# Two exchanges of an FFT convolution: from moves inside SBUF to stores and loads through DRAM, with both frequency halves in one transform and a new plan of the order

## The chip, the cores and the metric

The kernel runs on one core of one Trainium2 chip. The metric is the device time of one execution in microseconds (us). A kernel is run several times, in rounds with the kernel before on the same chip; each execution also lists the mean clock that was granted to TensorE, as a share of full speed. Engines: PE is TensorE's matmul side, PEld its weight loads (they overlap), DVE is VectorE, ACT is ScalarE, POOL is GpSimd, SP is SyncE. All DMAs of this kernel are issued from SP's one queue, strictly in program order; "SPq" in the profile is that queue's issuing.

## The reference, cut to what matters

```python
def _A_ref(q, k, v, shift_k, ssm_k, ssm_D):        # S = 2048, D = 640
    # kv = (4-tap causal shift filter of k) * v
    kv_f = rfft(pad(kv, S));  kf_f = rfft(pad(ssm_k, S))     # length 2S, along the sequence
    y = irfft(kv_f * kf_f)[:, :S, :] + kv * ssm_D
    return q * y

def _B_ref(x, w1, w2, w3, w4):
    h = gelu(layernorm(x) @ w1)          # then a shift by one or two tokens, by column group
    x1 = x + shifted(h) @ w2
    return x1 + gelu(layernorm(x1) @ w3) @ w4      # w3: 640 x 1536

return g * a + (1 - g) * b               # a = _A_ref(x, ...), b = _B_ref(x, ...), x = A_q
```

The change touches the long convolution in `_A_ref`. The dense matmuls of `_B_ref` stay as they are and are there for PE to work on while the convolution waits.

## The kernel before

The 2048 tokens lie as 128 partitions (`P`) x 16 (`T1`); `D` is 640 channels and `DH` is half of them. A transform is done in two matmul stages. The first stage (`F1`) works on each of the 16 slices; then the data must be exchanged between partitions, because the second stage (`M3`, a 128x128 block matrix) needs, on one partition, what lay on 16 others. In a partition index `(a q)` of the first stage, `a` goes from 0 to 7 and `q` from 0 to 15; after the exchange the partitions are `(a, t)`.

Half of the channels (`dh`) and half of the frequencies (`h`) are taken at a time, so there are eight transforms: four of the filter (r = 0 to 3; results go to `HD` in DRAM), four of the data (r = 4 to 7; multiplied with the filter's and brought back by one stage into `VR`). After each pair of data transforms, an inverse needs a second exchange. Both exchanges are DMAs from SBUF to SBUF:

```python
    def gx(r):                       # first exchange: 16 moves of 80 KB in each of 8 transforms
        stage = (RA, RB)[r % 2]
        for k in range(T1):
            w = [k_s2[r - 1, k // 2]] if r else k_cj + k_f1
            k_gx[r, k] = dma(lambda k=k: GRt[:, k, :],
                             lambda k=k: stage.rearrange("(a q) t d -> a q t d", a=8)[:, k],
                             P * 640, 640, evs + w)          # evs: all eight evacuations of stage 1

    def inverse(dh):                 # second exchange: 16 moves of 160 KB for each of 2 inverses
        vdeps = [k_v[r, kp] for r in (4 + 2 * dh, 5 + 2 * dh) for kp in range(T1 // 2)]
        for tp in range(T1 // 2):
            vb = G.buf("pv")                                  # three slots
            for j in range(2):
                k_vx[dh, t1] = dma(lambda vb=vb, j=j: PV[:, vb.slot, j],
                                   lambda t1=t1: VR.rearrange("(a q) t h d -> a q t (h d)", a=8)[:, t1],
                                   P * 1280, 1280, vdeps + ns, take=[vb] if j == 0 else [])
            ...                                               # then the inverse's matmuls and evacuation
```

The order of instructions isn't written by hand. The kernel builds a graph of all operations, and a list scheduler, run when the kernel is built, plans it with cost constants and with a pair of priorities for each group of operations (`WANTED`). What it plans is the order in which each engine gets its instructions. The constants for DMAs:

```python
    def dma(self, nbytes, packet, deps, fn, take=(), give=()):
        n = self.add({"D": (0.6, 0.6)}, deps, lambda e: fn(), take, give)          # us to issue
        n.bytes = -(-nbytes // packet) / 16.0 * (0.03 * -(-packet // 4096) + packet / 27000.0)
    ...
                    if opts == "D" and len(dmas) >= 8 and dmas[-8] > now + 1e-9:   # eight in flight
                        continue
    ...
                    line = max(now + 1.9, line) + n.bytes     # every packet is shared by 16 engines
```

Of the kernel before, what the change touches and what calls it, by code (L numbers as in the profile page):

```python
# [30 lines left out]
class Graph:  # L31
# [21 lines left out]
    def dma(self, nbytes, packet, deps, fn, take=(), give=()):  # L53
        n = self.add({"D": (0.6, 0.6)}, deps, lambda e: fn(), take, give)
        n.bytes = -(-nbytes // packet) / 16.0 * (0.03 * -(-packet // 4096) + packet / 27000.0)
        return n
# [23 lines left out]
    def forward(self):  # L80
# [19 lines left out]
        while placed < len(nodes):  # L100
            while True:
# [25 lines left out]
                if n.bytes is not None:  # L127
                    line = max(now + 1.9, line) + n.bytes
                    fin = line + 0.7
                    dmas.append(fin)  # L130
# [36 lines left out]
    "tables": (668, 1861), "loads": (3010, 3397.5), "hT": (1054, 1150.5), "LN1": (1024.5, 1172.5),  # L167
    "W1": (851, 1958.5), "W1.0": (337, 568), "W1.1": (526, 633), "W1.2": (263, 1091), "W1.3": (213.5, 699),
    "gate": (287, 3792.5), "mixsh": (902.5, 1653.5), "W2": (504, 741.5), "ks": (1289, 2357), "I1": (463.5, 2277.5),
    "p0.1": (-20, 674), "p0.gx": (115.5, 1589.5), "p1.1": (2353, 3097.5), "p0.2": (79, 136), "p1.gx": (240.5, 432.5),  # L170
    "p2.1": (863.5, 950.5), "p1.2": (110.5, 958.5), "p2.gx": (71, 358), "p3.1": (64, 1032.5), "p2.2": (395, 975),
    "p3.gx": (297, 1420.5), "p4.1": (371, 969), "p3.2": (252.5, 1391), "p4.gx": (1472, 1553), "p5.1": (722, 1661),
    "p4.hh": (770, 1452.5), "p4.2": (1240, 1290), "p5.gx": (-20, 254.5), "p6.1": (63.5, 287.5),
    "p5.hh": (2300.5, 3013), "p5.2": (132, 300), "p6.gx": (1391.5, 2568), "inv0": (1209.5, 2253.5),
    "p7.1": (58, 174.5), "p6.hh": (2391, 2893.5), "p6.2": (432.5, 679), "p7.gx": (617.5, 3276.5),
    "p7.hh": (696, 1575.5), "p7.2": (454, 1231), "inv1": (550.5, 1330.5), "LN2": (1022.5, 1104.5),
    "LN2.0": (1284.5, 1692.5), "W3.0": (75, 243), "W4.0": (503, 2717), "LN2.1": (347, 952.5), "W3.1": (3658, 4180),
    "W4.1": (592.5, 2133), "LN2.2": (232.5, 368.5), "W3.2": (426, 2444.5), "W4.2": (1684.5, 1911.5),
    "LN2.3": (2004.5, 3650.5), "W3.3": (461, 634), "W4.3": (2785.5, 3746.5), "final": (3243.5, 4779.5),
# [11 lines left out]
def kernel(  # L191
# [16 lines left out]
    nc = tc.nc  # L208
# [26 lines left out]
    HT = big.tile([P, 2, T1, DH], BF16, name="HT")  # L235
    R3 = big.tile([P, T1, 2, DH], BF16, name="R3")
    R5 = big.tile([P, 2 * T1 * DH], BF16, name="R5")
    R4 = big.tile([P, FT * D], BF16, name="R4")
    GR = big.tile([P, T1 * DH], BF16, name="GR")
# [5 lines left out]
    XY = big.tile([P, 2, D], BF16, name="XY")  # L245
    XS = big.tile([P, 2, 2, DH], BF16, name="XS")
    PV = big.tile([P, 3, 2, 2, DH], BF16, name="PV")
    HST = big.tile([P, 2, 4, DH], BF16, name="HST")
    HD = dram.tile([4, P, T1 * DH], BF16, name="HD")
    PS = [psp.tile([P, 2, 512], F32, name="ps%d" % i) for i in range(4)]  # L250

    KN = R3.rearrange("p t e d -> p t (e d)")
    VR = R3
    HN = R5.rearrange("p (a t2 t1) -> p a t1 t2", a=DT, t1=T1)
    HNl = R5.rearrange("p (a t) -> p a t", a=DT)
    GRt = GR.rearrange("p (t d) -> p t d", t=T1)
    RA = R5[:, 0:T1 * DH].rearrange("p (t d) -> p t d", t=T1)
    RB = R5[:, T1 * DH:].rearrange("p (t d) -> p t d", t=T1)
    HH = HT
# [6 lines left out]
    CJB = GR[:, 0:4 * D]  # L266
# [10 lines left out]
    NANG = [R11[:, 4 * T1 * 130:4 * T1 * 130 + 2048].bitcast(I32), GR[:, 4 * D:4 * D + 2048].bitcast(I32)]  # L277
# [13 lines left out]
    G.pool("hst", 2)  # L291
    G.pool("xnt", 2)
    G.pool("gtp", 5)

    def cact(n):
        return (0.11 + n / 1300.0, 0.28 + n / 1300.0)
# [7 lines left out]
    def pe(cols, n=1):  # L304
        return n * max(0.066, 0.000472 * cols)
# [88 lines left out]
    for g in range(4):  # L394
# [3 lines left out]
        for j in range(4):  # L398
# [11 lines left out]
            parts.append(act(P, [k_s16, k_wv, k_small] + before, f_sin))  # L410
        k_and = dvec(0.7, parts, lambda g=g: nc.vector.tensor_scalar(
            out=NANG[g % 2], in0=NANG[g % 2], scalar1=8191, scalar2=None, op0=ALU.bitwise_and))
        k_f1.append(act(1024, [k_and], lambda g=g: nc.scalar.activation(
# [3 lines left out]

    M3 = cons.tile([P, 3, P], BF16, name="M3")
    prow = gtile(1, I32)
    k_prow = pool(0.1, [], lambda: nc.gpsimd.iota(prow, pattern=[[1, 1]], base=0, channel_multiplier=1))  # L420
    tr = gtile(3)
    tri = tr.bitcast(I32)

    def make_tr():
        for i, bits in enumerate((15, 48, 64)):
            nc.vector.tensor_scalar(out=tri[:, i:i + 1], in0=prow, scalar1=bits, scalar2=None, op0=ALU.bitwise_and)
        nc.vector.tensor_copy(out=tr, in_=tri)

    k_tr = dvec(0.4, [k_prow], make_tr)
    ck1, k_ck1 = iof(3 * P, ([[0, 24], [1, 16]], 0, 0))  # L430
    cof, k_cof = iof(3 * P, *(([[stp, 2], [0, 64]], b0, 0) for (stp, b0) in ((12, 12), (4, 12), (4, 8))))
    crm = gtile(3 * P)

    def make_crm():
        for m, val in enumerate((4.0 / 64, 8.0 / 64, 0.0)):
            nc.gpsimd.memset(crm[:, m * P:(m + 1) * P], val)

    k_crm = pool(0.85, [], make_crm)
    ckl, k_ckl = iof(P, ([[0, 2], [16, 4], [0, 16]], 0, 0))
# [3 lines left out]
    def make_an():  # L443
        nc.vector.scalar_tensor_tensor(out=an, in0=ck1, scalar=tr[:, 0:1], in1=cof, op0=ALU.mult, op1=ALU.add)
        nc.vector.scalar_tensor_tensor(out=ani, in0=crm, scalar=tr[:, 2:3], in1=an, op0=ALU.mult, op1=ALU.add)
        nc.vector.tensor_scalar(out=ani, in0=ani, scalar1=15, scalar2=None, op0=ALU.bitwise_and)
        nc.vector.tensor_scalar(out=ckl, in0=ckl, scalar1=tr[:, 1:2], scalar2=None, op0=ALU.is_equal)

    k_an = dvec(1.5, [k_tr, k_ck1, k_cof, k_crm, k_ckl], make_an)
    k_m3s = act(3 * P, [k_an], lambda: nc.scalar.activation(out=ck1, in_=ani, func=ACT.Sin, scale=PI / 8, bias=BPI[:]))  # L450

    def make_m3():
        for m in range(3):
            nc.vector.tensor_tensor(out=M3[:, m, :], in0=ck1[:, m * P:(m + 1) * P], in1=ckl, op=ALU.mult)
# [38 lines left out]
    for k in range(DT):  # L493
        k_w1m.append(pool(0.43, [l_w1], lambda k=k: nc.gpsimd.tensor_copy(
            out=W1M[:, k, :].rearrange("p (g c) -> p g c", g=4),
            in_=W1[:, k, :].rearrange("p (g c) -> p g c", g=4)[:, :, P:CG])))
    k_cj = []
    for j in range(4):
        k_cj.append(G.add({"G": (1.36, 1.43), "V": (0.47, 0.55)}, [l_cj], lambda e, j=j: (
# [38 lines left out]
    for p in range(8):  # L538
        ns = []
        for s in (2 * p, 2 * p + 1):  # L540
# [4 lines left out]
            ns.append(dvec(0.97, [l_q[s]], f_st))  # L545
# [117 lines left out]
    l_w3a = dma(lambda: W3[:, 0:3], lambda: w3v[:, 0:3], 3 * P * 3072, 3072, k_w1)  # L663
# [56 lines left out]
    for s in range(T1):  # L720
# [15 lines left out]
        k_x1.append(dvec(0.93, [k_w2[s]], f_x1, give=[b]))  # L736
        k_sq.append(G.add({"A": (0.8, 0.97)}, [k_x1[s]] + [n for (_, _, n) in k_mix], lambda e, s=s: nc.scalar.activation(  # L737
            out=JK, in_=QX[:, s, :], func=ACT.Square, accum_out=SQS[:, s:s + 1])))
    l_w3b = dma(lambda: W3[:, 3:5], lambda: w3v[:, 3:5], 2 * P * 3072, 3072, k_w2)
# [24 lines left out]
    l_w4 = dma(lambda: W4[:], lambda: B_w4.rearrange("(k p) e -> p k e", p=P), Fh * D * 2, 1280, kprev)  # L764

# [15 lines left out]
    k_gx = {}  # L781
    k_s2 = {}
    k_hd = {}
    k_pq = {}
    k_v = {}
    k_vx = {}
    k_inv = {}
    k_hh = {}
    k_s1 = {}
    l_qr = []  # L790
    stage_done = {}

    def pass1(r):
        G.tag = 'p%d.1' % r
        dh, h = divmod(r % 4, 2)
        ds = slice(dh * DH, (dh + 1) * DH)
        stage = (RA, RB)[r % 2]
        war = [k_gx[r - 2, k] for k in range(T1)] if r >= 2 else k_hn_free
        evs = []
        k_s1[r] = []  # L800
        for tp in range(T1 // 2):
            b = G.buf("ps")

            def f(b=b, tp=tp):
                for j in range(2):
                    t1 = 2 * tp + j
                    dt = r < 4 and t1 == 0
                    src = HT[:, dh, t1, :] if r < 4 else KV[:, t1, ds]
                    nc.tensor.matmul(P32(b)[:, j, 0:DH], lhsT=F1[:, t1, h, :], rhs=src, start=True, stop=not dt)  # L809
                    if dt:  # L810
                        nc.tensor.matmul(P32(b)[:, j, 0:DH], lhsT=F1[0:1, 0, h, :], rhs=DROW[:, ds], start=False,
                                         stop=True)
            deps = [k_f1[tp // 2]] + (k_ht[dh] + [l_d] if r < 4 else [k_ks[4 * dh + tp // 2]])
            t = ten(pe(DH, 2), deps + war, f, take=[b])
            k_s1[r].append(t)
            evs.append(evac(2 * DH, PSD, [t], lambda tp=tp: stage[:, 2 * tp:2 * tp + 2, :],
                            lambda b=b: P32(b)[:, :, 0:DH], give=[b]))
        stage_done[r] = evs

    def gx(r):  # L820
        G.tag = 'p%d.gx' % r
        stage = (RA, RB)[r % 2]
        evs = stage_done[r]
        for k in range(T1):
            w = [k_s2[r - 1, k // 2]] if r else k_cj + k_f1
            k_gx[r, k] = dma(lambda k=k: GRt[:, k, :], lambda k=k: stage.rearrange("(a q) t d -> a q t d", a=8)[:, k],
                             P * 640, 640, evs + w)

    def pass2(r):
        G.tag = 'p%d.2' % r  # L830
        h = r % 2
        for kp in range(T1 // 2):
            b = G.buf("ps")

            def f(b=b, kp=kp):
                for j in range(2):
                    nc.tensor.matmul(P32(b)[:, j, 0:DH], lhsT=M3[:, 0, :], rhs=GRt[:, 2 * kp + j, :], start=True,  # L837
# [219 lines left out]
```

## Time and profile before

| kernel before | |
|---|---|
| median of three executions | 315.14 us (310.18 to 316.18) |
| profiled execution | span 312.4 us, granted clock 0.961 |
| all later executions beside other kernels | 309 to 315 us, mostly labelled fast |

In profiles a tile has the program's name with a buffer number: here `R_72` holds the first stage's results (`RA`, `RB`) and `R_71` holds `VR`; `ps_85` to `ps_88` are PSUM buffers. The page of the profile has these lines (busy time, share of the span and instructions of each engine; the DMA engines' busy share and the rate in the third part):

```profile
span 312.4 us, 4773 instructions
...
PE 250.7 (80%) x1690; PEld 153.5 (49%) x1690; DVE 181.0 (58%) x343; ACT 182.2 (58%) x261; POOL 45.9 (15%) x127
...
DMA packets 41745, 54.73 MB, mean 175 GB/s; under 512 B 4986, under 2 KB 34427, under 8 KB 41722
...
q1 hardware_dynamic: 41722, 54.44, 62.5%
...
PE 38%; DMA 27%; SPq 10%; ACT 10%; DVE 8%; issue 5%; POOL 1%; ACTq 0%; DVEq 0%
```

No engine is full, and the chain of waits (last line) runs through PE for only 38% of the span. DMA and the queue's issuing hold 37% of it. The next lines give what the queue does: for each kind of transfer its count, and the shortest, median and longest time in ns to issue one.

```profile
L337 SPq DMA_DIRECT2D GR<-R_72 x128: 589/599/3366, 45.4 to 254.5; - x128
L337 SPq DMA_DIRECT2D PV<-R_71 x32: 589/622/1667, 203.4 to 299.1; - x32
...
L337 SPq DMA_DIRECT2D HD<-HST x16: 321/452/936, 55.3 to 156.3; - x16
```

The exchange moves (`GR`, `PV`) take 0.59 us at the least, the plain store of a whole tile (`HD`) 0.32 us. PE's longest waits for DMAs of the exchanges (us in total, times, longest):

```profile
PE ps_87 L913 <- DMA PV<-R_71: 9.9, 4, 6.8
PE ps_88 L913 <- DMA PV<-R_71: 5.2, 3, 3.3
PE ps_86 L837 <- DMA GR<-R_72: 3.5, 3, 2.4
...
PE ps_86 L913 <- DMA PV<-R_71: 3.0, 1, 3.0
...
PE ps_85 L913 <- DMA PV<-R_71: 1.2, 2, 1.0
```

The four `PV` lines are 19.3 us: PE stands before the inverse. And the chain of waits near the end shows how (start us, length us, what): one move lands after 5.52 us, two matmuls run, and the queue issues the next moves.

```profile
276.76 5.52 DMA PV<-R_71
...
282.32 0.45 PE ps_88 L913 x2
282.77 0.58 SPq L337
...
283.41 0.60 SPq L337
```

Of each line the first number is the window, the second its length, and the last three are the granted clock, the busy share of the 16 DMA engines, and GB/s:

```profile
46.00:52.50 6.50, 5.83 (x59) 3.41 (x57) 6.36 (x13) 4.95 (x7) 0.00 (x0) 1.00 0.42 87
247.00:255.00 8.00, 8.00 (x47) 4.42 (x46) 2.48 (x3) 6.26 (x9) 0.00 (x0) 1.00 0.45 105
271.00:281.00 10.00, 8.06 (x48) 4.47 (x46) 2.23 (x4) 1.50 (x3) 0.00 (x0) 1.00 0.42 100
```

In these stretches the busy share stays at 0.42 to 0.45 and the rate at about 100 GB/s.

### The profile page before, as it was taken

How to read it: one execution, taken by the hardware profiler on the slowest of the kernel's cores; microseconds unless marked ns; L12 is line 12 of the kernel's file. 1: busy time of each engine (PE TensorE's matmuls, PEld its weight loads, DVE VectorE, ACT ScalarE, POOL GpSimd, SP SyncE). 2: the span in 40 equal slices, each digit the busy share in tenths (PEclk: the TensorE clock that was granted, in tenths of full speed). 3: DMA queues.
4: the chain of work that ended last, by engine and by line, in shares of the span. 5: the costliest groups of instructions: out<-in, count | busy, mean ns of one | idle time of the engine just before them, and what ended most of it. 6: DMA issues, size and time to landing. Idle time of an engine off the chain costs nothing.

```text
span 312.4 us, 4773 instructions
## 1 busy us (share of the span) xinstructions
PE 250.7 (80%) x1690; PEld 153.5 (49%) x1690; DVE 181.0 (58%) x343; ACT 182.2 (58%) x261; POOL 45.9 (15%) x127
## 2 busy tenths in 40 slices
PE   0297788889969896989959799965879999977845
PEld 0283345446646552546636455532546566645522
DVE  7899779969876899341313553211358145336733
ACT  8677888766856995886848688510215677410000
POOL 5877300003674310000000000000000000000000
PEclk9997999999997999999989999996999999999987
DMA  7999805657455299695585899647641836045561
GB/s 252 405 316 370 309 7 105 154 163 185 87 154 173 102 239 264 171 316 159 145 221 143 203 219 261 150 113 210 163 102 35 196 77 166 14 119 157 147 187 52
DMA packets 41745, 54.73 MB, mean 175 GB/s; under 512 B 4986, under 2 KB 34427, under 8 KB 41722
## 3 DMA queue, kind: packets, MB, share of 16 engines
q1 hardware_dynamic: 41722, 54.44, 62.5%
q8 instruction: 13, 0.21, 0.3%
q14 instruction: 10, 0.08, 0.1%
HBM read 30.31 MB, written 7.86 MB: 122 GB/s over the span
## 4 chain that ended last, share of the span: by engine, by line
PE 38%; DMA 27%; SPq 10%; ACT 10%; DVE 8%; issue 5%; POOL 1%; ACTq 0%; DVEq 0%
DMA GR<-R_72 11%; SPq L337 10%; DMA PV<-R_71 8%; PE ps_86 L987 5%; ACT R_72 L327 4%; DMA R_73<-in_B_w_dram 3%; PE ps_85 L1004 3%; PE ps_85 L987 3%; DVE BST L543 2%; DMA HT<-HD 2%; PE ps_86 L1004 2%; PE ps_88 L726 2%; PE ps_87 L631 2%; PE ps_86 L726 2%; PE ps_87 L1004 1%
## 5 line engine op out<-in xcount | busy, mean ns | idle before, releaser
L1004 PEld LDWEIGHTS <-R_79 128*128 128x128 bf16 x384 | 39.1, 102 | 20.1 <-DMA R_73<-in_B_w_dram 1.5
L862 DVE TENSOR_TENSOR PV<-XS,HT 128x1280 bf16<-128x1280 bf16 x32 | 25.9, 824 | 29.5 <-ACT XS L327 27.0
L987 PEld LDWEIGHTS <-R_77 128*128 128x128 bf16 x240 | 23.3, 98 | 24.5 <-issue 4.0
L987 PE MATMUL ps_86<-XNT,R_77 128*128 128x512 bf16 x100 | 24.8, 379 | 3.6 <-ACT HST L329 3.1
L993 ACT ACTIVATE R_79<-ps_86 128x1024 bf16<-128x1024 f32 x10 | 10.2, 1023 | 25.8 <-PE ps_86 L987 20.9
L756 DVE TENSOR_TENSOR R_73<-R_71,R_73 128x1280 bf16<-128x1280 bf16 (+3 forms) x32 | 23.9, 757 | 0.1
L580 PEld LDWEIGHTS <-XY 128*128 128x128 bf16 x160 | 12.2, 106 | 22.1 <-DVE XY L572 17.3
L1004 PE MATMUL ps_85<-R_73,R_79 128*128 128x320 bf16 x120 | 21.0, 327 | 1.0 <-DMA R_73<-in_B_w_dram 1.0
L726 PEld LDWEIGHTS <-R_79 128*128 128x128 bf16 x160 | 16.1, 101 | 10.7 <-issue 4.3
L759 DVE TENSOR_TENSOR R_73<-R_73 128x1280 bf16<-128x1280 bf16 x24 | 19.8, 823 | 0.5
L809 PEld LDWEIGHTS <-F_75 128*128 128x128 bf16 x128 | 12.4, 100 | 15.5 <-issue 8.2
L913 PEld LDWEIGHTS <-I_76 128*128 128x128 bf16 x64 | 6.4, 103 | 25.2 <-issue 21.4
L837 PEld LDWEIGHTS <-M_95 128*128 128x128 bf16 x128 | 12.3, 98 | 10.8 <-issue 2.3
L987 PE MATMUL ps_85<-XNT,R_77 128*128 128x512 bf16 x70 | 17.4, 379 | 0.0
L1004 PE MATMUL ps_86<-R_73,R_79 128*128 128x320 bf16 x96 | 17.2, 330 | 0.0
L327 ACT CAST R_72<-ps_85 128x640 bf16<-128x640 f32 x20 | 14.1, 705 | 3.7 <-PE ps_85 L809 3.4
L631 PEld LDWEIGHTS <-R_77 128*128 128x128 bf16 x100 | 9.8, 101 | 13.1 <-issue 5.9
L1004 PE MATMUL ps_88<-R_73,R_79 128*128 128x320 bf16 x96 | 15.0, 299 | 0.0
L543 DVE BATCH_NORM_STATS2 BST<-QX 128x6 f32<-128x320 bf16 x32 | 13.7, 471 | 0.0
L737 ACT ACTIVATE I_76<-QX 128x640 bf16<-128x640 bf16 x16 | 11.8, 737 | 3.1 <-DVE QX L734 2.9
L919 DVE SCALAR_TENSOR_TENSOR KV<-ps_87,G_113,KV 128x320 bf16<-128x320 f32 x10 | 5.1, 547 | 14.1 <-PE ps_87 L913 13.9
L1014 DVE SCALAR_TENSOR_TENSOR QX<-ps_88,OMG,QX 128x640 bf16<-128x640 f32 x4 | 3.5, 884 | 16.3 <-PE ps_88 L1004 11.1
(188 smaller groups left out, 554.8 us busy)
## 6 DMA issues: line engine op xcount, KB each, us to landing
GR<-R_72 SPq DMA_DIRECT2D x128, 80.0 KB
HD<-HST SPq DMA_DIRECT2D x16, 320.0 KB
HT<-HD SPq DMA_DIRECT2D x8, 640.0 KB
HT<-HD SPq DMA_DIRECT2D x16, 320.0 KB
PV<-R_71 SPq DMA_DIRECT2D x32, 160.0 KB
R_72<-in_A_ssm_k_dram SPq DMA_DIRECT2D x5, 512.0 KB
R_71<-in_A_k_dram SPq DMA_DIRECT2D x4, 640.0 KB
KV<-in_A_v_dram SPq DMA_DIRECT2D x4, 640.0 KB
```

Source lines behind the costliest of these rows:

```text
L327: nc.scalar.copy(out=out(), in_=in_())
L337: return G.dma(nbytes, packet, deps, lambda: nc.sync.dma_start(out=out(), in_=in_()), **kw)
L543: nc.vector.bn_stats(out=BST[:, s % 4, j, :], in_=QX[:, s, j * DH:(j + 1) * DH])
L631: nc.tensor.matmul(P32(b)[:, j, :], lhsT=lhsT, rhs=XNT[:, xb.slot, k, :], start=(k == 0), stop=(k == DT - 1))
L726: nc.tensor.matmul(P32(b)[:, j, 0:DH], lhsT=gst_ap(k, s), rhs=W2[:, k, j * DH:(j + 1) * DH], start=(k == 0), stop=(k == DT - 1))
L756: lambda dst=dst, src=src, a=a, b=b, j=j, ds=ds: nc.vector.tensor_tensor(out=dst[:, a:b], in0=src, in1=CJ[:, j:j + 1, ds].to_broadcast([P, ...
L759: kprev = [dve(4 * DH, TWO, kprev, lambda dst=dst: nc.vector.tensor_tensor(out=ACC[:], in0=ACC[:], in1=dst[:], op=ALU.add))]
L809: nc.tensor.matmul(P32(b)[:, j, 0:DH], lhsT=F1[:, t1, h, :], rhs=src, start=True, stop=not dt)
L837: nc.tensor.matmul(P32(b)[:, j, 0:DH], lhsT=M3[:, 0, :], rhs=GRt[:, 2 * kp + j, :], start=True, stop=True)
L862: k_pq[r, kp] = dve(4 * DH, TWO, [n] + k_hh[r, kp // 4] + war, lambda xb=xb, vb=vb, kp=kp: nc.vector.tensor_tensor(out=PV[:, vb.slot], in0 ...
L987: nc.tensor.matmul(P32(b)[:, j, :], lhsT=W3[:, k, f * P:(f + 1) * P], rhs=XNT[:, xb.slot, k, :], start=(k == 0), stop=(k == DT - 1))
L1004: nc.tensor.matmul(P32(b)[:, j, 0:DH], lhsT=GTP[:, gbs[f // 4].slot, f % 4, i * P:(i + 1) * P], rhs=W4[:, f, j * DH:(j + 1) * DH], start=( ...
```

## The change

Its intent: send both exchanges through DRAM in whole-tile stores and loads with larger packets; take both halves `h` in one transform, so that four transforms are left and a packet of the first exchange is 1280 bytes; and pay for the room with small rings of stage buffers (`SG`, four slots). The cost constants of the scheduler and all priorities are new as well.

```diff
     def dma(self, nbytes, packet, deps, fn, take=(), give=()):
-        n = self.add({"D": (0.6, 0.6)}, deps, lambda e: fn(), take, give)
-        n.bytes = -(-nbytes // packet) / 16.0 * (0.03 * -(-packet // 4096) + packet / 27000.0)
+        n = self.add({"D": (0.45, 0.45)}, deps, lambda e: fn(), take, give)
+        n.bytes = -(-nbytes // packet) / 16.0 * (0.012 + packet / 21500.0)
-                    line = max(now + 1.9, line) + n.bytes
+                    line = max(now + 1.1, line) + n.bytes
 WANTED = {                       # all priorities replaced (cut)
-    GR = big.tile([P, T1 * DH], BF16, name="GR")
+    SG = big.tile([P, 4, 2, DH], BF16, name="SG")
+    XD = dram.tile([4, T1, P, D], BF16, name="XD")
+    VD = dram.tile([2, T1, P // T1, T1, D], BF16, name="VD")
     ...                          # more cost constants, M3's order of partitions (cut)
+    # stage 1, slice t1: both halves h, evacuated to a slot of SG, then one store of 160 KB
+            k_st1[r, t1] = dma(lambda t1=t1: XD[r, t1],
+                               lambda sb=sb: SG[:, sb.slot].rearrange("p h d -> p (h d)"), ...)
+    # before stage 2: four loads of 640 KB in each of four transforms
+        k_gr[r, c] = dma(lambda: GRt[:, (4 * r + c) % 3].rearrange("p k h d -> p (k h d)"),
+                         lambda: XD[r].rearrange("t (a q) f -> (t a) (q f)", q=T1)[:, 4*c*D:(4*c+4)*D],
+                         P * 5120, 5120, deps)
+    # second exchange: stores of 320 KB from HST as the products come, then loads of 320 KB
+                k_vd[dh, k // 2] = dma(lambda k=k: VD[dh].rearrange("t a q f -> (t a) q f")[:, k-1:k+1], ...)
+            ld = dma(lambda i=i: VX[i % 4].rearrange("p t h d -> p t (h d)"),
+                     lambda tp=tp: VD[dh, 2*tp:2*tp+2].rearrange("t a q f -> (a q) t f"), P * 2560, 1280, ...)
```

## The prediction

> **What bounds the kernel now.** No engine is full. The busy shares give PE 80%, DVE 58%, ACT 58%, DMA 62.5%. Matmul counts times their spacing in the chain of waits (0.27 us per pair of 320 columns, 1.08 us per five of 512) give an estimate of 239 us of PE work; the span is 312.4 us. Of the 70 us lost, by PE's order, about 22 go before 54 us (first loads, layer-norm), 9 up to the first W3 matmul at 114 us (ACT and DVE mostly 0.8-0.98 busy, windows), about 40 after it.
>
> Those 40 us belong to the exchanges. In the chain, SBUF-to-SBUF GR moves hold 11%, PV moves 8.4% and the DMA queue's issuing 10%. Each of the 128 GR and 32 PV moves takes 0.59-0.62 us to issue, often 1.1 us, so between 157 and 202 us the queue issues almost without a break. PE waits for PV 19 us in all (6.8 us at 214 us, 2.9 at 228, several stops from 276 to 304). After the last second-stage matmul (270 us) the kernel needs 42 us, for about 25 us of PE work: eight pairs of PV moves pass three slots, interleaved with output stores.
>
> **What changes.** Matmul and evacuation counts stay. 128 GR moves of 80 KB become 64 stores of 160 KB and 16 loads of 640 KB; 32 PV moves become 16 stores and 16 loads of 320 KB. Plain moves issue in 0.33-0.45 us. DMA issues fall from about 261 to 219, exchange issues from 160 to 112. Bytes rise: 10.5+5.2 MB cross twice, so 54.4 becomes about 70 MB, packets 41.7k about 34k. Rates from the windows: 640-byte packets about 237 GB/s (0.043 us each), 1280-byte about 320, 5 KB about 358. Estimate: 73 us of 16-engine time removed, about 110 added, DMA busy 195 becomes about 230 us, near 79% of the new span. So the gain is not bandwidth; it is issues, wider pieces (at most eight transfers are in flight) and looser coupling.
>
> Cost: every exchange now lands in DRAM before its load. The Trainium skill (DMA: Bandwidth & Descriptors, "Anatomy of one DMA") gives about 2 us fixed per DMA, mostly completion, on another issue path; this trace has 4.35 us for an HD store and 3.1-3.8 us for GR. I estimate 8 us from the last evacuation to the first loaded chunk, four times instead of eight, mostly covered: PE's order has 11 us of work between the last matmul of the first inverse's input and that inverse, and 7 us at the second. The four SG slots tie evacuation to stores landing.
>
> **Gain, estimate.** Middle V exchange -8 us, tail -9 us, queue-bound stretch and GR waits of 155-202 us -8 us, new stalls behind DRAM and SG +4 us..
>
> **Predicted: 291 us, 8 in 10 within 280 to 306. Faster by over 2%: 0.80; within 2%: 0.12; slower: 0.08.**
>
> **Right if** PE stays near 250 us busy while its idle time falls; the inverse's wait for DMA falls from 19 to under 8 us; the tail after the last second-stage matmul is about 33 us; DMA busy is 75-82% with about 70 MB; exchange lines hold under 20% of the chain.
>
> **Wrong if** the queue, strictly in order, blocks stores behind loads that wait; ACT stops for SG slots (waits for XD stores over 10 us); the DMA saturates after 115 us; or the throttle takes the denser PE work down (mean clock now 0.961).

## The result

| | before | after |
|---|---|---|
| executions, us | 310.18, 315.14, 316.18, 314.00 | 273.71, 279.09, 273.06, 278.95 |
| median | 314.57 | 276.33 |
| fast executions of after | | 273.06 and 273.71, clock 0.999 and 1.0 |
| profiled span | 312.4 us, clock 0.961 | 271.9 us, clock 1.0 |

The ratio of the fast runs is 0.876, with a 95% interval of 0.8525 to 0.8995. A ratio here is the mean time of one kernel's fast runs over that of the other's fast runs of the same rounds, so it is not quite the ratio of the medians. The direction was predicted, but the gain is nearly twice as large as predicted: 276.33 us lies below the interval of 280 to 306.

The same lines of the profile's page after the change:

```profile
span 271.9 us, 4747 instructions
...
PE 236.6 (87%) x1675; PEld 149.9 (55%) x1690; DVE 186.7 (69%) x362; ACT 175.0 (64%) x250; POOL 46.8 (17%) x125
...
DMA packets 34690, 70.47 MB, mean 259 GB/s; under 512 B 5610, under 2 KB 22763, under 8 KB 34666
...
q1 hardware_dynamic: 34666, 70.17, 79.4%
...
PE 43%; DMA 24%; ACT 7%; issue 2%; DVE 2%; SPq 2%; ACTq 0%; POOL 0%; DVEq 0%
```

Bytes (70 MB), packets (34,700) and the DMA share (79%) came out as predicted. The queue's issuing fell from 10% of the chain to 2%. The issue times (line 336 is the helper's line now):

```profile
L336 SPq DMA_DIRECT2D XD<-SG x64: 319/324/1606, 28.6 to 138.0; - x64
...
L336 SPq DMA_DIRECT2D R_71<-XD x16: 319/326/813, 69.6 to 215.1; - x16
...
L336 SPq DMA_DIRECT2D VD<-HST x16: 319/325/411, 181.9 to 244.9; - x16
```

A transfer of two to eight times the bytes takes 0.32 us to issue, about half (the 16 loads of the second exchange, with three dimensions, take 0.36 at the least). Over the whole kernel SP spends 99.9 us issuing instead of 187.0 (the sum of all DMA instructions' durations on SP; such a duration can contain waiting, as gronly shows below). In the kernel after, `R_71` holds what `XD` is loaded to, and `R_71` and `CJB` what `VD` is loaded to. PE's waits for the loads of the exchanges are down to 3.5 us:

```profile
PE ps_87 L843 <- DMA R_71<-XD: 1.4, 2, 0.9
...
PE ps_89 L924 <- DMA R_71<-VD: 1.3, 2, 0.8
...
PE ps_89 L924 <- DMA CJB<-VD: 0.8, 1, 0.8
```

And the chain of waits after the last second-stage matmul (243.8 us) is PE work, with the inverse's matmuls (line 924) put between the dense ones:

```profile
245.13 0.54 PE ps_90 L924 x4
245.67 1.08 PE ps_87 L999 x5
246.75 1.09 PE ps_88 L1016 x8
...
254.35 0.56 PE ps_88 L924 x4
254.91 0.02 issue
254.93 6.72 DMA R_71<-VD
```

The tail from that matmul to the end fell from 42.3 us to 28.1 us (33 was predicted). The load at 254.93 us is on the chain, but PE had other work in that time.

Windows in which the exchange runs, here together with other transfers, show what the prediction had not seen (columns as before):

```profile
130.00:140.00 10.00, 9.95 (x61) 5.45 (x60) 2.95 (x6) 6.98 (x9) 0.00 (x0) 1.00 1.05 377
140.00:150.00 10.00, 10.00 (x80) 7.24 (x79) 3.16 (x6) 5.03 (x6) 0.00 (x0) 1.00 1.05 347
```

The busy share is 1.05 (above 1: the packet records of these windows add up to slightly more than the time of 16 engines) and the rate 347 to 377 GB/s, against 0.42 to 0.45 and 87 to 105 GB/s before. I counted from the trace's packet records how many packets were in flight at once, every 20 ns in those windows:

| window | in flight, mostly | packets, median ns |
|---|---|---|
| before, 46 to 52.5 us (first exchange) | 6 to 9, peak at 8 | 640 B: 52 |
| before, 271 to 281 us (second exchange) | 6 to 9, peak at 8 | 1280 B: 96 |
| after, 130 to 140 us | 16 and more | 1280 B: 55; 2560 B: 102; 5120 B: 196 |

By this count the old moves used eight of the 16 engines. The Trainium skill (DMA: Bandwidth & Descriptors, "Why a DMA increments its semaphore by 16 and not by 1", the paragraph on how many engines) says that the number of engines is the largest number up to 16 that divides the size of the slowest dimension of both access patterns. The old source has an outer dimension of 8; the trace agrees, with eight packets in flight. In these windows each packet was also slow: 96 ns for 1280 bytes against 55. Not everywhere, though: over all stretches in which only the old moves have packets of that size, a quarter of the 640-byte packets take 32 ns or less and a quarter of the 1280-byte ones 55 or less, and the means are 45 and 82 ns. An estimate from mean durations, packets times their time over the engines at work: the old exchanges need 16,384 x 45 ns / 8 + 4,096 x 82 ns / 8 = 134 us of the queue's transfers. The new ones need, with 8,192 packets of 1280 B (57 ns) and 2,048 of 5120 B (281 ns) in the first, and 2,048 of 2560 B (108 ns) and 4,096 of 1280 B (66 ns) in the second, 96 us on 16 engines (a few other transfers have packets of these sizes, and are in these means). Twice the bytes go through in about seven tenths of the time. Issuing limits the old way as well: one move of 80 KB every 0.6 us is, as an estimate, at most 137 GB/s.

### The profile page after: what moved, and what is told of

It reads as the page before. It is cut to its first block, busy times and chain, and to the rows that moved or that the text cites. A ratio compares the mean times of both kernels' runs of the same rounds, so it can differ in the third digit from the quotient of the medians.

```text
span 271.9 us, 4747 instructions
## 1 busy us (share of the span) xinstructions
PE 236.6 (87%) x1675; PEld 149.9 (55%) x1690; DVE 186.7 (69%) x362; ACT 175.0 (64%) x250; POOL 46.8 (17%) x125
## 3 DMA queue, kind: packets, MB, share of 16 engines
q1 hardware_dynamic: 34666, 70.17, 79.4%
## 4 chain that ended last, share of the span: by engine, by line
PE 43%; DMA 24%; ACT 7%; issue 2%; DVE 2%; SPq 2%; ACTq 0%; POOL 0%; DVEq 0%
DMA XD<-SG 6%; DMA VD<-HST 5%; PE ps_88 L1016 5%; DMA HD<-HST 5%; DMA R_71<-VD 4%; PE ps_89 L999 4%; PE ps_89 L1016 4%; DMA R_71<-XD 3%; PE ps_88 L999 3%; PE ps_90 L1016 2%; PE ps_87 L1016 2%; PE ps_87 L999 2%; PE ps_90 L999 2%; ACT SG L326 2%; SPq L336 2%
## 5 line engine op out<-in xcount | busy, mean ns | idle before, releaser
L1016 PEld LDWEIGHTS <-R_77 128*128 128x128 bf16 x384 | 37.5, 98 | 16.9 <-issue 1.1
L865 DVE TENSOR_TENSOR PV<-XS,R_70 128x1280 bf16<-128x1280 bf16 x32 | 25.7, 822 | 22.8 <-ACT XS L326 20.8
L999 PEld LDWEIGHTS <-R_75 128*128 128x128 bf16 x240 | 23.2, 98 | 22.3 <-issue 2.0
L999 PE MATMUL ps_89<-XNT,R_75 128*128 128x512 bf16 x95 | 24.4, 379 | 0.6 <-ACT R_77 L1005 0.3
L587 PEld LDWEIGHTS <-XY 128*128 128x128 bf16 x160 | 11.5, 103 | 18.1 <-DVE XY L579 13.9
L733 PEld LDWEIGHTS <-R_77 128*128 128x128 bf16 x160 | 15.6, 98 | 10.1 <-issue 2.1
L813 PEld LDWEIGHTS <-F_73 128*128 128x128 bf16 x128 | 12.3, 97 | 14.2 <-issue 6.7
L766 DVE TENSOR_TENSOR R_72<-R_72 128x1280 bf16<-128x1280 bf16 x24 | 19.7, 821 | 0.3
L1016 PE MATMUL ps_87<-R_72,R_77 128*128 128x320 bf16 x120 | 18.7, 299 | 0.1
L843 PEld LDWEIGHTS <-M_97 128*128 128x128 bf16 x128 | 12.2, 98 | 11.4 <-issue 2.6
L876 PEld LDWEIGHTS <-M_97 128*128 128x128 bf16 x128 | 12.5, 98 | 7.1 <-issue 0.9
L326 ACT CAST SG<-ps_87 128x640 bf16<-128x640 f32 x21 | 14.6, 693 | 2.4 <-PE ps_87 L813 1.9
L1016 PE MATMUL ps_88<-R_72,R_77 128*128 128x320 bf16 x96 | 15.0, 299 | 0.7 <-ACT HST L328 0.7
L638 PEld LDWEIGHTS <-R_75 128*128 128x128 bf16 x100 | 9.4, 97 | 10.7 <-issue 2.0
L999 PE MATMUL ps_88<-XNT,R_75 128*128 128x512 bf16 x58 | 14.8, 379 | 0.1
L1016 PE MATMUL ps_90<-R_72,R_77 128*128 128x320 bf16 x96 | 14.5, 299 | 0.0
L587 PE MATMUL ps_87<-IDN,XY 128*128 128x128 bf16 x30 | 3.2, 249 | 11.8 <-DVE XY L579 11.8
L999 PE MATMUL ps_90<-XNT,R_75 128*128 128x512 bf16 x46 | 11.9, 379 | 1.1 <-ACT XNT L326 0.7
```

What stands on the lines that cost most here:

```text
L326: nc.scalar.copy(out=out(), in_=in_())
L587: nc.tensor.transpose(out=P16(b)[:, j, k * P:(k + 1) * P], in_=XY[:, x.slot, k * P:(k + 1) * P], identity=IDN[:])
L733: nc.tensor.matmul(P32(b)[:, j, 0:DH], lhsT=gst_ap(k, s), rhs=W2[:, k, j * DH:(j + 1) * DH], start=(k == 0), stop=(k == DT - 1))
L766: kprev = [dve(4 * DH, TWO, kprev, lambda dst=dst: nc.vector.tensor_tensor(out=ACC[:], in0=ACC[:], in1=dst[:], op=ALU.add))]
L813: nc.tensor.matmul(P32(b)[:, h, 0:DH], lhsT=F1[:, t1, h, :], rhs=src, start=True, stop=not dt)
L843: nc.tensor.matmul(P32(b)[:, h, 0:DH], lhsT=M3[:, 0, :], rhs=GRt[:, (4 * r + k // 4) % 3, k % 4, h, :], start=True, stop=True)
```

## The experiments

Theory A says that the exchanges (engines at work and issue time) were the brake; the expectations of k8, st8 and iss2 hold a narrower A, the engines alone. Rivals: C, the packets' size alone; B, only fewer issues; D, the new constants and priorities of the planner alone; E, the merged halves and the small rings. Eleven kernels were run. Those that are edits of the kernel after (k8, st8, iss2, p640, ld2, ring2) keep its planned order, so their losses contain what a fixed order loses when its transfers get slower. Those that are edits of the kernel before (replan, gronly, gronly2, both) had their priorities searched anew under the new constants.

### k8: the kernel after with its first exchange on eight engines

```diff
-    XD = dram.tile([4, T1, P, D], BF16, name="XD")
+    XD = dram.tile([4, T1, 8 * (T1 + 1) + 1, D], BF16, name="XD")      # a pad row splits the pattern
-    k_st1[r, t1] = dma(XD[r, t1], ...)
+    k_st1[r, t1] = dma(XD[r, t1, 0:8 * (T1 + 1)].rearrange("(a q) f -> a q f", a=8)[:, 0:T1], ...)
-    k_gr[r, c] = dma(GRt[...], XD[r]... , P * 5120, 5120, deps)        # one load
+    k_gr[r, c] = dmas([(GRt[64*i:64*i+64, ...], xv[8*i:8*i+8]) for i in range(2)], ...)   # outer dim 8
```

> The changed kernel with the first exchange (64 stores, 16 loads) forced onto 8 of the 16 DMA engines: rows in DRAM are padded so that the access pattern's outer dimension is 8, the loads go in two halves of 64 partitions. Same order on every engine, same packets (1280 and 5120 B), 16 issues more. Theory A (the old SBUF-to-SBUF moves were slow because they ran on 8 engines, 8 packets in flight in the trace of before): 8 packets in flight in the exchange's windows, a 640 KB load takes about 3 us longer, and the time goes up by 8 to 20 us over the changed kernel (273.4 us of its fast runs). Rival B (issues and packet size made the difference, engines did not): at most 3 us more.

Measured: 326.95 us median; fast runs 323.68 and 323.80; ratio to before 1.0385 [1.0202, 1.0567]. This is about 50 us more than the kernel after. The same windows as above:

```profile
130.00:140.00 10.00, 8.29 (x47) 4.29 (x47) 7.37 (x12) 6.53 (x9) 0.00 (x0) 1.00 0.46 152
140.00:150.00 10.00, 4.96 (x26) 2.36 (x25) 4.79 (x9) 4.46 (x5) 0.00 (x0) 0.94 0.63 178
```

The busy share is back at 0.46 in the first window (0.63 in the second, with other transfers), and mostly eight packets are in flight. Engines matter, more than A had expected; rival B (at most 3 us) fell. But the SP queue also issues 28 us longer than in the kernel after (128.1 us), and the loads are halves, so a control was needed (ld2).

### ld2: the control of k8, loads in halves on 16 engines

```diff
+    k_gr[r, c] = dmas([(GRt[64*i:64*i+64, ...], xv[64*i:64*i+64]) for i in range(2)], ...)   # XD not padded
```

> Control of run k8: the changed kernel with its 16 loads of the first exchange in two halves of 64 partitions, on 16 engines. Theory A: at most 5 us over the changed kernel, so nearly all of k8's 50 us belongs to the engines. If the splitting was to blame in k8: 20 us or more.

Measured: 283.07 us (281.20 to 284.47), ratio 0.905 [0.8986, 0.9114]: about 10 us more than the kernel after, twice what was expected, but 40 us less than k8. Sixteen more issues cost 8 us of issuing (108.0 instead of 99.9 us on SP): a half load takes 0.59 us to issue (median), a whole one 0.33. A part of the 40 us may be the clock, 0.94 in k8's fast runs and 0.99 to 1.0 in ld2's; why it differs is not shown. The Trainium skill (DMA: Bandwidth & Descriptors, "Rules for kernel authors") advises against splitting a transfer by partition halves; this run agrees, with its 10 us.

### st8: only the stores on eight engines

```diff
-    XD = dram.tile([4, T1, P, D], BF16, name="XD")
+    XD = dram.tile([4, T1, 8, T1 + 1, D], BF16, name="XD")
+    k_st1[r, t1] = dma(XD[r, t1, :, 0:T1], ...)          # loads: still 16 engines, one piece
```

> The same padding for the 64 stores alone, loads as in the changed kernel; no issue more. Theory A: a store takes about 0.5 us longer to land and evacuations wait longer for SG slots (7.3 us in the changed kernel), 2 to 6 us more in all. Rival B: within 1 us of the changed kernel.

Measured: 287.11 us; fast runs 285.69 to 287.33; ratio 0.9195 [0.9077, 0.9312]; 13 us more than the kernel after, with the same number of issues (224). The stores' issue time went from 0.32 to 0.57 us, so engines and issue time come together here: the pattern with an outer dimension of eight is dearer in both. (p640 below takes them apart.) ACT's wait for `SG` slots rose from 7.3 to 12.2 us. The number is twice the expected one.

### iss2: every transfer of the exchanges in two halves

```diff
+    for i in range(2):       # stores and loads of both exchanges: partitions 64*i to 64*i+63
+        nc.sync.dma_start(out=out[i], in_=in_[i])
```

> The changed kernel with every exchange transfer split into two halves of 64 partitions: 112 issues more (219 becomes 331), still 16 engines, same packets, same order on the other engines. Rival B (the number of issues of the strictly ordered queue bounds): 112 more at 0.33 us are 37 us more queue time; the time goes up by 8 us or more. Theory A: issues are slack now, at most 3 us more.

Measured: 303.96 us (301.61 to 305.27), ratio 0.9742 [0.9622, 0.9863]; 30 us more. So issues matter as well, and the narrower theory A, engines alone, fell. The 112 more issues raised SP's issuing from 99.9 to 182.7 us, as long as before the change (187.0): a half store takes 0.55 us to issue (median), not the 0.33 of the expectation. The run splits every transfer besides, so that the same number of transfers in flight holds half the bytes, and SP waits 52 us for DMAs instead of 40; so the 30 us need not be issue time alone. Fifteen or more packets were in flight for 59% of the time after 40 us, against 26% in the kernel before (65% in the kernel after): with all engines but with the old issuing time, the gain is 2.6% instead of 12.4%.

### p640: packets of 640 bytes on 16 engines

```diff
-    XD = dram.tile([4, T1, P, D], BF16, name="XD")
+    XD = dram.tile([4, T1, P, 2, 400], BF16, name="XD")  # a gap after each 640 bytes
```

> The changed kernel with 640 B packets in the first exchange both ways (the two halves of a row lie apart in DRAM), 16 engines, no issue more. Rival C (large packets made the gain): at 0.042 us per 640 B packet the DMA needs an estimated 18 us more of all 16 engines' time, and the kernel 8 us or more. Theory A: 2 to 5 us more; the three-dimensional stores may also issue in 0.6 us in place of 0.32.

Measured: 284.07, 283.88, 283.44 (slow) and 277.62 us (fast); 4 to 5 us more than the kernel after in the same state. Rival C, which needed 8, fell. The "larger packets" of the change's intent are worth little: on 16 engines 640-byte packets take 36 ns in the mean, against 45 in the old moves. The Trainium skill (DMA: Bandwidth & Descriptors, "Why small descriptors are slow (HBM only)") says that moves within SBUF don't suffer from small packets; the old moves were slow for another reason.

This run is also a control for issue time. The stores here have three dimensions and take as long to issue as those of st8; the first line is p640, the second st8:

```profile
L336 SPq DMA_DIRECT2D XD<-SG x64: 512/564/3243, 28.5 to 144.9; - x64
L336 SPq DMA_DIRECT2D XD<-SG x64: 570/583/1371, 28.5 to 148.9; - x64
```

SP issues 135.2 us in all (st8 115.9, k8 128.1, the kernel after 99.9), and yet the loss is 4 to 5 us, against 13 in st8 and 50 in k8. So dear issues alone do not make those losses: about 8 of st8's 13 us, and by p640 and ld2 together an estimated 35 of k8's 50, are left for the eight engines and what a fixed order makes of them.

### ring2: two slots of SG instead of four

```diff
-    SG = big.tile([P, 4, 2, DH], BF16, name="SG")
+    SG = big.tile([P, 2, 2, DH], BF16, name="SG")        # slot % 2 in the evacuation and the store
```

> The changed kernel with two SG slots in place of four, same order on every engine. A store takes 2.7 us to land, so two slots let an evacuation through every 1.4 us in place of 0.7: where first stages run densely, evacuations wait; 8 to 20 us more. If the ring is no constraint: under 2 us.

Measured: 313.16 us; fast runs 310.15 to 313.38; ratio 1.0045 [0.9964, 1.0126]; 38 us more, twice what was expected, so that all of the gain is gone. ACT's first wait here, and then the same wait in the kernel after:

```profile
ACT SG L326 <- DMA XD<-SG: 40.3, 19, 6.9
```

```profile
ACT SG L326 <- DMA XD<-SG: 7.3, 5, 4.9
```

The store of a slot lands 2.7 us after its issue (median in the kernel after), and ACT can't evacuate PSUM before. Four slots nearly cover that, two don't.

### replan: the kernel before, with new constants and new priorities only

```diff
-        n = self.add({"D": (0.6, 0.6)}, ...)
-        n.bytes = ... / 16.0 * (0.03 * -(-packet // 4096) + packet / 27000.0)
+        n = self.add({"D": (0.45, 0.45) if ways == 16 else (0.6, 0.6)}, ...)
+        n.bytes = ... / ways * (0.012 + packet / 21500.0) * (1.0 if ways == 16 else 1.3)
+        # ways=8 on the moves of both exchanges; the other constants as in the kernel after; WANTED searched anew
```

> The kernel before with its exchanges as they were (SBUF to SBUF, 8 engines, 160 moves), but planned anew: the scheduler's cost constants of the changed kernel, the old moves costed as 8 engines and 0.6 us an issue, and its priorities searched again (100,000 trials). Rival D (the new plan, not the exchange, made the gain): below 290 us. Theory A (exchange): 300 us or more, within 4% of before.

Measured: 296.59 us (295.98 to 297.37), ratio 0.9487 [0.9432, 0.9542]. Between the two theories: the plan alone is worth 16 us, and the other 23 us of the change need its exchanges. Here the transfers are the old ones, but the order has work ahead of them, and PE's total wait for `GR` and `PV` falls from 24.6 to 7.0 us. The line of the inverse:

```profile
PE ps L916 <- DMA PV<-R: 4.4, 4, 3.0
```

Was it the search or the constants? I also searched the old priorities under the old constants (two searches of 61,000 trials) and found nothing better than the plan that the kernel had. That plan's makespan under the old constants is 278.4 us; the chip took 314. Under the new constants, which know the eight engines, the makespan of replan is 294.4 us and the chip took 296.6. These makespans are the scheduler's own numbers and no chip times. They suggest that the old plan was as good as its constants allowed, and that the constants were wrong about the exchange; no run has the new constants without new priorities.

### gronly: the kernel before with only its first exchange through DRAM

```diff
-            k_gx[r, k] = dma(GRt[:, k, :], stage.rearrange("(a q) t d -> a q t d", a=8)[:, k], ...)
+            st.append(dma(XD[r, ts].rearrange("t p d -> p t d"), stage[:, ts, :], P * 1280, 640, [evs[tp]]))
+            n = dma(GR[:, 4*c*DH:(4*c+4)*DH],
+                    XD[r].rearrange("t (a q) d -> (t a) (q d)", q=T1)[:, 4*c*DH:(4*c+4)*DH], P * 2560, 2560, st + w)
-            VR.rearrange("(a q) t h d -> a q t (h d)", a=8)[:, t1]      # 8 source partitions, 16 apart
+            VR.rearrange("(t a) k h d -> t a k (h d)", a=8)[t1]         # 8 neighbouring ones
```

> The kernel before with the first exchange alone taken through DRAM (64 stores of 160 KB in 640 B packets, 32 loads of 320 KB in 2560 B packets, all on 16 engines), but still eight half transforms, the old stage buffers and the old second exchange; planned anew in the same way as the run replan. Theory A: 275 to 290 us, most of the gain. Rival E (merging both k2 halves and the small rings are what pays): 298 us or more.

Measured: 298.60 us (297.84 to 300.34), ratio 0.9558 [0.9497, 0.9619]. Theory A's 275 to 290 was missed. The last edit, taken over from the kernel after with its `M3`, had made the second exchange slower: its 1280-byte packets took 108 to 175 ns (means of stretches of 10 us between 190 and 270 us) instead of 69 to 104 in the kernel before. One of its moves took 1.69 us to issue (median), in gronly2 0.62, with as many moves and 0.60 and 0.59 at the least: here the issuing grew along with the slower transfers. PE waited for it:

```profile
PE ps L933 <- DMA PV<-R: 17.4, 8, 3.9
```

Up to the first inverse the run is as good as the kernel after (see the table of lags below), so the test was confounded and was repeated.

### gronly2: the same, with the second exchange's partitions as before

```diff
-            VR.rearrange("(t a) k h d -> t a k (h d)", a=8)[t1]
+            VR.rearrange("(a q) t h d -> a q t (h d)", a=8)[:, t1]      # and M3's columns to fit
```

> The kernel before with its first exchange through DRAM on sixteen engines, still eight half transforms, its second exchange left as it was (moves within SBUF, source partitions spaced by 16 as in the kernel before, which gronly had changed by mistake), new plan. Theory A (half the engines and dear issues in the first exchange cost most of what a new plan alone leaves): 278-290 us, lag up to the first inverse below 30 us, 1280-byte packets of the second exchange back at 70-110 ns. Rival E (the merging of the halves and the second exchange give the rest): 292 us or more, as gronly's 298.6.

Measured: 281.48 us (281.12 to 283.77), ratio 0.9027 [0.8964, 0.9089]. A's interval holds it. PE's wait for the second exchange is 3.0 us:

```profile
PE ps L932 <- DMA PV<-R: 3.0, 3, 1.2
```

(The lag at the first inverse is met too, 28.3 us. The packets of the second exchange have a median of 99 ns between 193 and 200 us, within the 70 to 110 expected.) Eight half transforms are still there, so the first exchange's way through DRAM is worth about 14 us on top of the plan.

### both: eight half transforms, both exchanges through DRAM

```diff
+            if h == 1:           # after gronly: store what both halves left in VR, 320 KB
+                k_vd[r // 7, kp] = dma(VD[r // 7, :, 2*kp:2*kp+2].rearrange("p k f -> p (k f)"), VR[:, 2*kp:2*kp+2]..., P * 2560, 2560, ...)
+            ns = [dma(PV[:, vb.slot]..., VD[dh].rearrange("(t a) k f -> t (a k) f", a=8)[2*tp:2*tp+2]..., P * 2560, 1280, vdeps, take=[vb])]
```

> The kernel before with both exchanges through DRAM on sixteen engines (stores and loads of the second one as in the kernel after, 320 KB each), but still eight half transforms, 640-byte pieces in the first exchange and the buffers of before; new plan. Theory A (engines and issues of the exchanges, plus the new plan, are the whole gain): 270-281 us, so within 3% of the kernel after, tail after the last second-stage matmul below 32 us. Rival E (both k2 halves in one transform and the small stage rings hold a part of the gain of their own): 285 us or more.

Measured: 266.60 us (265.71 to 269.09), ratio 0.8548 [0.8483, 0.8612]. It is faster than theory A asked for and faster than the kernel after, and rival E fell: no gain of the merged halves and the small rings is seen, neither here nor in best, which has them and is level with this run. The tail is 28.9 us. Its page:

```profile
PE 238.4 (90%) x1690; PEld 151.1 (57%) x1690; DVE 180.1 (68%) x351; ACT 181.8 (69%) x259; POOL 48.2 (18%) x127
...
PE 69%; DVE 11%; DMA 8%; POOL 6%; issue 3%; ACT 1%; SPq 1%; DVEq 0%; POOLq 0%; ACTq 0%
```

PE is 90% busy, and the chain of waits runs through PE for 69% of the span and through DMA for only 8%.

### best: the kernel after with its priorities searched again

```diff
 WANTED = {          # two searches of 78,000 trials under its own constants; nothing else changed
```

> The kernel after with only its priorities searched anew under its own cost model (model makespan 262.4 instead of 264.5). If the model ranks plans at this level: 270-274 us, ratio to before about 0.865. If the model's last per cent means nothing on the chip: 273-279 us as the kernel after, or worse.

Measured: 267.68 us (266.99 to 268.88, six executions), ratio 0.8557 [0.8498, 0.8616]. It is faster than both expectations: the scheduler's makespan fell by only 2.1 us (264.5 to 262.4), the chip's time by about 6, fast against fast. So a single plan carries luck of that size, and steps of the table below are to be read with it in mind. best and both have overlapping intervals. Every execution of either is faster than every one of the kernel after, but the latter was run in other rounds, and its interval (0.8525 to 0.8995) overlaps with theirs.

### The table of lags

The lag of an event is its time minus the ideal PE work that stands before it in PE's order (0.216 us for a matmul of 512 columns, 0.136 for 320, 0.107 for a transpose, from the spacings in the chain of waits). It rises where PE loses time. The 0.107 is wrong: it is what the chain shows at 27 and at 95 us of the run before, where the clock was 0.5 (five transposes in 0.53 us); the median spacing is 0.056 in the kernels before and after. So all lags are too small, by 8 us in the first column and 14 in the last, but nearly alike in every kernel: compare within a column. (The prediction's 239 us of PE work comes out with the same figure; with 0.056 it is about 226.)

| kernel | first W2 matmul | first W3 | first inverse | last second stage | end |
|---|---|---|---|---|---|
| before | 22.4 | 28.0 | 42.3 | 55.9 | 73.1 |
| after | 13.2 | 23.7 | 26.2 | 27.9 | 32.6 |
| replan | 28.7 | 41.4 | 44.9 | 45.1 | 55.4 |
| gronly | 20.0 | 23.5 | 24.6 | 35.4 | 56.7 |
| gronly2 | 22.9 | 26.8 | 28.3 | 34.2 | 40.0 |
| both | 19.2 | 19.5 | 18.8 | 19.7 | 24.6 |
| k8 | 14.1 | 38.0 | 84.0 | 86.8 | 91.0 |

With 0.056 for a transpose the kernel before loses about 48 us from the first W3 matmul on, the kernel after 12, both 8. With gronly the loss comes only after the first inverse begins, where its second exchange is slow; k8 loses its time while the first exchange runs.

## Why the prediction was wrong

The mechanism's direction was right and the counts were right; the size was not. The step that failed is the sum under "Gain, estimate": its four terms make about -21 us, from a span of 312.4 to 291. In the steps of the experiments, as ratios to before in fast runs:

| step | ratio | worth of about 313 us |
|---|---|---|
| new constants and priorities (replan) | 0.9487 | -16 us |
| first exchange through DRAM (gronly2) | 0.9027 | -14 us |
| second exchange through DRAM (both) | 0.8548 | -15 us |
| merged halves, small rings, the plan of the change (after) | 0.876 | +7 us |

The steps were taken in this one order; in another the shares could differ. The last one lies within overlapping intervals.

Point by point:

- **The missing term.** The sum has no term for the cost constants and the priorities, though the diff replaces all of them. Measured: 16 us. It is the largest single error. Added to the sum, it would have made about -37, which is 275 us.
- **"So the gain is not bandwidth; it is issues, wider pieces ... and looser coupling."** Half wrong. The rate behind it, "640-byte packets about 237 GB/s", came from windows in which exchanges and ordinary loads ran together. The time of a packet was right (43 ns in the mean over the run before), but the rate takes 16 of them at once; with eight it is half, and where the first exchange runs nearly alone the trace has 87 GB/s with eight packets in flight. k8 puts the first exchange back on eight engines and loses 50 us where its control ld2 loses 10 and p640, with issues as dear, 4 to 5; that the engines count is shown for the kernel after. Issues count as well: iss2 keeps 16 engines and loses 30 us. For the old moves themselves the two were not separated: no run gives them 16 engines at their old number of issues.
- **The three terms of the exchanges** (-8, -9, -8 us: -25 in all) were about right in size: the two steps measured make -29, before the +7 of the last step. That is in part luck. The reason was only half right, and the new plan alone (replan) takes most of the waits that these terms counted, 24.6 to 7.0 us of PE's waits for `GR` and `PV`, while the exchanges brought 29 us on top of it.
- **"New stalls behind DRAM and SG +4 us."** The wait is there, ACT stands 7.3 us for `SG` slots, below the limit of 10 that the prediction set. What the last step costs is near it, 7 us; but best shows that it is the plan that the change came with, as the same program with other priorities is level with both.
- **"PE stays near 250 us busy."** Wrong: 236.6 us. Busy time includes the clock: a pair of 320-column matmuls takes 0.53 us at 95.9 us of the run before, where the clock is 0.5, and 0.27 elsewhere. The profiled run before had a mean clock of 0.961, with 0.89 between 210 and 240 us and 0.71 from 300 us on, and 250.7 x 0.961 = 241; the run after had 1.0. The fear that denser PE work would lower the clock wasn't met. The profiled runs with a span over 294 us have 0.937 to 0.969, those under 286 us 0.981 to 1.0. Why is not shown. An estimate of the part of the gain that can have come that way: in the profiled runs of before, replan, gronly2, both and after PE was busy at clock 0.5 for 21.4, 19.2, 9.8, 6.0 and 0 us, and half of this is lost. So the clock can hold about 11 us of the whole change, and about 1, 5 and 2 us of the three steps.
- **What held:** the inverse's wait for DMA under 8 us (2.1); DMA busy 75 to 82% with about 70 MB (79.4%, 70.5 MB); the tail (33 predicted, 28.1 measured). "Exchange lines under 20% of the chain" just held: by line the chain has XD<-SG 6.5%, VD<-HST 5.4%, R_71<-VD 4.5% and R_71<-XD 3.3%, together 19.7%. (HD<-HST, 4.7% more, is the store of the filter's spectrum, which both kernels have.)
- **The latency of a landing.** The Trainium skill (DMA: Bandwidth & Descriptors, "Anatomy of one DMA") has about 2 us fixed on another issue path. Here 160 KB stores land after 2.7 us and 640 KB loads after 5.1 us (medians in the kernel after), so the assumed 8 us for store and load was right. Little of it shows as waits of PE (3.5 us in all), since other work was in line.
- **The start.** The lag at the first W2 matmul fell by 9 us, which the prediction didn't have. Neither both (19.2) nor best keeps all of it (18.4 us there), and both are faster; so it's a choice of that plan and not what the gain rests on.

What stays open: the split between engines and issue time in the old moves, why the clock differs, and how far the steps carry plan luck, which best puts at about 6 us for one kernel.

## What to carry to other kernels

Read the DMA rate of a suspected transfer only in windows where it runs alone, and look at the busy share and at the packets in flight there: here a share of 0.42 with eight packets in flight, while the queue went on issuing, came from an outer dimension of 8 in one of the two patterns; twice the bytes over 16 engines were quicker. When a diff also replaces the constants and priorities of a planner, give that a term of its own in the sum and run the old program with the new plan as the first experiment. On an in-order queue with stages of a few us, the number of buffers and of issues decides as much as bandwidth: two slots in place of four, or 112 more issues, took back all of the gain or three quarters of it.

## What the Trainium skill lacked or had wrong

- DMA: Bandwidth & Descriptors has no figure, pattern by pattern, for what one plain DMA costs the issuing SP queue. Measured: 0.32 us at the least for a whole 128-partition tile in two dimensions, 0.44 for half loads (ld2), 0.51 for whole stores in 640-byte pieces (p640), 0.57 to 0.59 us for patterns with an outer dimension of 8. It calls the time to initiate a DMA usually small relative to the DMA ("Issuing engines are not separate DMA queues"). For one move this holds (0.59 us beside 3 to 4 us for most `GR` moves on the chain), but the sum was 187.0 of 312 us; 83 us more of it go with a loss of 30 us (iss2), 35 us more with 4 to 5 (p640).
- The same page's rule for the number of engines stands among its "Rules for kernel authors" too, as "Use all 16 engines"; the prediction drew on that page and passed it over. The page has no figure for what it costs in a kernel: k8 costs 50 us by it, ld2, its control, 10. It holds for moves inside SBUF too (eight in flight for an outer dimension of 8).
- "Why small descriptors are slow (HBM only)" says that moves within SBUF don't suffer the small-packet penalty. What it doesn't say is that a source of eight partitions can make them slower than the way over DRAM: 1280-byte packets took 82 ns in the mean against 57 where the stores to DRAM run, and 108 to 175 ns where the eight partitions were neighbours (gronly).
- "Rules for kernel authors" says of halves by partition "Don't bother"; the runs make it stronger: 10 us for 16 transfers (ld2), 30 us for 112 (iss2).
